# Sums by TensorE in five chunks only, a weight matrix stored by column group, and a new order, in a three-stage sequence kernel

## The chip, the cores and the metric

The kernel runs on one core of one Trainium2 chip. The metric is the device time of one execution in microseconds (us). The time of a version is the median of its runs.

## The reference, cut to what matters

The input has B = 4 sequences of S = 768 positions, H = 8 heads of D = 48 columns (8 * 48 = 384 = DM). Three stages follow one another.

```python
# 1: a recurrence with decay w and a bonus u, per head
cur   = outer(u * k[t], v[t])
y[t]  = r[t] @ (state + cur)
state = w[t][:, None] * state + outer(k[t], v[t])
# 2: four attention experts (64 columns each), two picked per position
a   = softmax(causal(scale * q_e @ k_e.T))
out += weight_e * (a @ v_e @ wo_e)
# 3: channel mix
xn  = (x - mu) / sqrt(var + 1e-6) * g_ln
out = x + relu(xn @ w_ch1) @ w_ch2        # 384 -> 1536 -> 384
```

Everything is float32; the kernel must stay near that precision, so most products are made from a high and a low float16 part of each operand, in three passes.

## The kernel before, in words

**Stage 1** (`rwkv_chunk`) works on chunks of 128 positions: 6 per sequence, 24 in all, numbered n = 6 b + c. Scans on VectorE make the running products of the decay (lines 801 and 816); TensorE then makes, per chunk, the matrix of products of r and k (`mm_a`, line 918, tile `pa`), the part of the output that comes from the state (`mm_inter`, line 954), the part within the chunk (`mm_intra`, lines 968 and 970) and the chunk's own addition to the state (`mm_d`, line 983, tile `pd`). A copy under a mask (`am_copy`, line 925) puts the products above the diagonal of the tile `am`, on whose diagonal GpSimd has written the bonus (`mk_bonus`, line 891).

The bonus of a position and head, sum over d of r k u, is made in one of two ways. For chunks n < NCB (8 before), GpSimd multiplies the transposed r and k of the chunk (`mk_rk`, line 847), TensorE sums over the partitions by 8 small matmuls against u (`mm_cb`, line 853, tile `pcb`) and ScalarE copies the 8 columns out (line 858). For the others, a transfer of 384 KB brings r and k by position (`load_q`, line 796, tile `tok`, of which there is one buffer), GpSimd multiplies them and then by u (lines 862 and 872), and VectorE sums (line 877). The u for this second way is loaded by `load_u` at chunk n = NCB.

The state goes from chunk to chunk in one of two ways as well. ScalarE multiplies the old state by the chunk's decay (`mk_dec`, line 910). Where `whole` is true (0 < c < 5 and n < NST, 10 before: chunks 1 to 4 and 7 to 9), TensorE adds that product to the chunk's own part in PSUM, by a matmul with the identity (line 979), and the next `mk_dec` reads the PSUM bank, which stays taken until then. In the other chunks two VectorE additions do it (line 998; copies at line 996 where c = 0), and the bank is free after them.

**Stage 2** (`project`, `attend`) makes q, k, v and the gates of a sequence (lines 1123 and 1188), the scores (line 1302), the softmax on ScalarE and VectorE, a transposing transfer, and the products with v and wo (lines 1387 and 1439).

**Stage 3** (`norm`, `mlp`) takes two blocks of 128 positions at a time: 18 matmuls per pair of column blocks with the first matrix (`mm_1`, line 1532, tile `pm`), 6 per step with the second (`mm_2`, line 1565, tile `pz`). There are 12 such pairs of blocks.

**The weights** w1 and w2 (each 384 x 1536 numbers) are read at the start as 64-bit words, because the matrices come as float64, in sets: w1 in 4 sets of 3 parts of 384 columns, w2 in 6 sets of 2 parts. VectorE unpacks a set in three passes over it (`decode`, lines 505, 506 and 507: `unpack` is a tensor_scalar, the other two are scalar_tensor_tensor). In the stored w1, part 4 kk + f holds row block kk and column group f, so that a set (one f, three kk) takes every fourth place. ScalarE takes the square sum of a set for its scale (line 575), and each part is then split in a high and a low half (lines 632 to 667; for w1 by a matmul with a diagonal, line 655).

**What sets the order.** All engines' instructions are written in one order worked out before compilation by `Plan.order`. It simulates the engines with the duration written beside each operation (`@op("PE", 0.85, ...)`). At each step it takes the operations that could start within LOOK of the earliest one of an engine, and among them the one with the smallest due time plus LATE times its delay; due times are sums of the entries of the table PLACE for the operation's group and name. Buffers come in rings (SIZES, for instance `tok=1`, PSUM ring `r=3`). Until the time UNTIL it may put in spare matmuls that only keep TensorE awake (`spin`, line 744), by the rule of SPAN, LEAST and GAP. So a change of PLACE or of a written duration changes the order of instructions on every engine and in SyncE's queue of transfers.

Of the kernel before, what the change touches and what calls it, by code (L numbers as in the profile page):

```python
# [20 lines left out]
P = 128  # L21
# [5 lines left out]
KK = DM // P  # L27
# [10 lines left out]
PRM = dict(LOOK=0.0, LATE=1773.6262, UNTIL=43.8356, SPAN=6.2999, LEAST=0.0732, GAP=2.1085, LAND=2.27, NPA=6, NQ=1, NCB=8, DIRECT=('w2',), NST=10)  # L38
PLACE = {
# [21 lines left out]
    ('o', 3, 5): -698477.53, ('proj', 0): -295018.27, ('proj', 0, 's'): -125022.81, ('proj', 0, 1): 80220.25,  # L61
    ('proj', 0, 2): -21343.01, ('proj', 1): -177643.56, ('proj', 1, 1): -107377.99, ('proj', 1, 2): -196040.46,
    ('proj', 2): -91098.53, ('proj', 2, 1): 13642.21, ('proj', 2, 2): -449346.82, ('proj', 3): 93391.83,
# [12 lines left out]
    ('vals', 0, 1): 35417.3, ('vals', 0, 2): -24875.8, ('vals', 1): -89872.89, ('vals', 2): 21146.28,  # L76
# [7 lines left out]
    ('w2', 8): 67189.64, 'a_den': -27933.93, 'a_hi': -151558.33, 'a_lo': 225945.59, 'a_of': -8012.47,  # L84
    'a_sum': 90213.0, 'a_tr': -81147.68, 'ae': 9532.96, 'am_copy': 126573.78, 'f_flag': -83856.37,
    'f_rows': 359040.86, 'f_turn': 39994.68, 'f_w': 28227.87, 'forth': 248281.69, 'g_exp': 19442.15,
    'g_norm': -38900.58, 'g_peak': -151938.75, 'g_rank': 230355.43, 'hi': 134007.83, 'less': -136319.44,
    'lo': -225283.24, 'load': -122866.37, 'load_g': -30043.72, 'load_k': -57046.71, 'load_q': -279458.56,
    'load_r': -217492.83, 'load_u': -13561.36, 'load_ut': 56724.36, 'load_v': 141804.62, 'm_hi': -262991.62,
    'm_lo': 122988.52, 'm_out': -32307.81, 'm_store': 132697.31, 'mk': 33523.95, 'mk_begin': 34263.89,  # L90
    'mk_bonus': -306653.38, 'mk_cb': -154529.96, 'mk_dec': -93213.35, 'mk_diag': -197725.73, 'mk_k2': 294244.16,
    'mk_k2t': 81775.2, 'mk_rk': -143861.49, 'mk_rp': -291319.24, 'mk_ruk': -96442.3, 'mk_sd': -340521.47,
    'mk_side': 120524.29, 'mk_tot': 228284.39, 'mm_1': 319489.06, 'mm_2': 191970.76, 'mm_a': -77276.6,
    'mm_av': -163565.22, 'mm_cb': 11831.02, 'mm_d': -269837.93, 'mm_inter': -24853.46, 'mm_intra': -48830.3,
    'mm_k': -8197.28, 'mm_o': 142200.91, 'mm_q': -177202.8, 'mm_s': -59954.25, 'mm_v': -130717.65, 'mt': -15383.65,
    'n_hi': -5943.82, 'n_lo': -146399.19, 'n_root': -31312.6, 'n_tr': 121898.14, 'n_var': -147654.16,
    'n_xn': -111826.26, 'o1': 140934.93, 'o2': -234884.57, 'o3': 6748.89, 'o4': -239856.13, 'o5': 93661.14,
    'o_mean': 273629.77, 'o_st': 120380.94, 'o_x1': -222100.87, 'q_hi': 140529.69, 'q_less': 98224.57,
    'q_lo': 97584.28, 's_bias': -108185.03, 's_exp': 5623.4, 's_hi': 119074.81, 's_lo': 11657.8, 's_max': 72228.32,
    's_tr': 53618.26, 'scan': 180273.48, 'se': -288101.94, 'stack_k': 117902.0, 'stack_q': 35533.64,  # L100
    'state': -226076.38, 'times': 63945.68, 'top': 19104.78, 'unpack': -157479.11, 'unpack2': 157371.31,
    'unpack3': 101864.41, 'v_hi': 188866.74, 'v_lg': -140728.23, 'v_lo': 25317.14, 'vc': -144449.83,
    'w_check': 22598.42, 'w_sane': 282903.73, 'ws_hi': 30208.09, 'ws_less': -128406.54, 'ws_lo': -66728.24,
# [200 lines left out]
NR = KK * DF // RW  # L304
# [1454 lines left out]
```

## Time and profile before

| | |
|---|---|
| median of 3 runs | 630.76 us (630.12 to 631.0) |
| the profiled execution's own time | 629.59 us |
| its span | 627.3 us |
| TensorE (PE) busy | 598.3 us, 95% of the span |
| VectorE (DVE) busy | 427.4 us, 68% |
| ScalarE (ACT) busy | 386.0 us, 62% |
| GpSimd (POOL) busy | 140.1 us, 22% |

The span is the time from the first to the last recorded instruction, and 2.3 us of the execution lie around it. PEld is TensorE's loading of weights, which overlaps its matmuls. A group of instructions is named by its line, engine and operation, with the tiles it writes and reads; L853 is line 853. PEclk is the clock that TensorE was granted, 1.00 being 2.4 GHz and 0.50 being 1.2 GHz.

### The profile page before, as it was taken

The numbers are of one execution on the slowest core, as the hardware profiler recorded it, in microseconds if no ns is written. First come the engines' busy times: TensorE is split into PE (matmuls) and PEld (weight loads), VectorE is DVE, ScalarE is ACT, GpSimd is POOL, SyncE is SP. The second block draws the span as 40 slices with busy tenths as digits, with TensorE's granted clock in tenths as the row PEclk, the third lists the DMA queues.
The fourth block names the chain that finished last, engine by engine and source line by source line (L and its number), as shares of the span: only waits on it lengthen the run. The fifth ranks groups of instructions, "written<-read, shape, count | busy, mean of one in ns | idle before, by whom it ended". The sixth has DMA issues, their size and how long they took to land.

```text
span 627.3 us, 16254 instructions
## 1 busy us (share of the span) xinstructions
PE 598.3 (95%) x6593; PEld 440.9 (70%) x6594; DVE 427.4 (68%) x808; ACT 386.0 (62%) x1062; POOL 140.1 (22%) x176
## 2 busy tenths in 40 slices
PE   6589899899999999999999999999999999999996
PEld 3357566677668866876877676776886768687783
DVE  5978788988978588888874898674464555542220
ACT  5367889876765586776656777573464756343120
POOL 4613043333644034325400232000000000000000
PEclk8659999899999999999999999999999999999999
DMA  8623764698996488739754767626228454522000
GB/s 279 228 101 124 191 168 128 130 226 212 193 215 123 93 217 162 186 81 248 168 84 103 194 128 162 112 56 121 48 43 152 93 102 85 100 62 60 14 14 31
DMA packets 150706, 82.15 MB, mean 131 GB/s; under 512 B 123616, under 2 KB 136672, under 8 KB 150624
## 3 DMA queue, kind: packets, MB, share of 16 engines
q1 hardware_dynamic: 150624, 81.03, 56.5%
q8 instruction: 54, 0.88, 0.6%
q14 instruction: 28, 0.23, 0.1%
HBM read 41.16 MB, written 4.72 MB: 73 GB/s over the span
## 4 chain that ended last, share of the span: by engine, by line
PE 72%; ACT 12%; DVE 10%; issue 3%; DMA 2%; SPq 0%; POOL 0%; ACTq 0%; DVEq 0%
PE pz L1565 21%; PE pm L1532 18%; PE pq L1123 7%; PE ps L1302 5%; PE po L1387 4%; PE px L1439 3%; ACT ps L1344 3%; PE pa L918 3%; PE py L968 2%; PE py L954 2%; PE pv L1188 1%; PE pk L936 1%; ACT hl L1360 1%; PE pd L983 1%; DMA xnT<-in_w_dram 1%
## 5 line engine op out<-in xcount | busy, mean ns | idle before, releaser
L1565 PE MATMUL pz<-w_w,hid 128*128 128x384 f16 x864 | 151.0, 326 | 0.2 <-DVE hid L1547 0.2
L1532 PE MATMUL pm<-xnT,w_w 128*128 128x256 f16 x1296 | 149.9, 273 | 0.2 <-DVE hid L1547 0.2
L1532 PEld LDWEIGHTS <-w_w 128*128 128x128 f16 x1296 | 124.8, 98 | 17.1 <-issue 1.7
L1565 PEld LDWEIGHTS <-hid 128*128 128x128 f16 x864 | 81.9, 98 | 50.7 <-issue 1.8
L1364 DVE SCALAR_TENSOR_TENSOR hl<-ps,hl 128x512 f16<-128x512 f32 (+2 forms) x68 | 54.7, 812 | 33.7 <-ACT hl L1360 33.0
L1547 DVE SCALAR_TENSOR_TENSOR hid<-pm,hid 128x512 f16<-128x512 f32 x72 | 49.3, 687 | 37.7 <-ACT hid L1543 37.6
L1543 ACT ACTIVATE hid<-pm 128x512 f16<-128x512 f32 x72 | 42.8, 594 | 50.8 <-PE pm L1532 50.7
L1481 POOL TENSOR_TENSOR rs_y<-rs_v,half 128x2 f32<-128x2 f32 x12 | 9.4, 780 | 229.6 <-ACT rs_v L1477 229.6
L1123 PE MATMUL pq<-xT,w_qk 128*128 128x256 f16 x432 | 51.8, 273 | 0.5 <-ACT qs L1148 0.5
L1360 ACT ACTIVATE hl<-ps 128x512 f16<-128x512 f32 (+2 forms) x68 | 46.7, 696 | 4.9 <-DMA pt<-hl 3.6
L1344 ACT ACTIVATE ps<-ps,bias 128x640 f32<-128x640 f32 (+1 forms) x32 | 26.2, 820 | 37.1 <-DVE ps L1315 34.1
L1123 PEld LDWEIGHTS <-w_qk 128*128 128x128 f16 x432 | 41.7, 98 | 6.9 <-issue 1.3
L891 POOL TENSOR_SCALAR_AFFINE_SELECT am<-cb 128x512 f32<-128x512 f32 x48 | 34.7, 745 | 40.2 <-DVE cb L877 26.2
L833 POOL TENSOR_TENSOR rp<-seq,fw 128x512 f32<-128x512 f32 x24 | 30.6, 1273 | 51.0 <-DVE fw L816 42.5
L1387 PEld LDWEIGHTS <-pt 128*128 128x128 f16 x1008 | 37.2, 99 | 5.6 <-DMA pt<-hl 1.0
L1387 PE MATMUL po<-vt,pt 128*128 128x64 f16 x1008 | 40.3, 194 | 0.6 <-DMA pt<-hl 0.5
L1572 DVE SCALAR_TENSOR_TENSOR x<-pz,ioutFalse,x 128x384 f32<-128x384 f32 x24 | 14.7, 614 | 36.7 <-PE pz L1565 36.7
L1315 DVE TENSOR_SCALAR_CACHE_REDUCE ps<-ps,scales 128x640 f32<-128x640 f32 (+1 forms) x32 | 30.6, 956 | 12.8 <-PE ps L1305 12.7
L1344 ACT ACTIVATE ps<-ps,bias,scales 128x128 f32<-128x128 f32 (+3 forms) x64 | 37.9, 591 | 1.8
L925 DVE COPY_PREDICATED am<-above,pa 128x512 f32<-128x512 int8 x48 | 33.0, 723 | 4.3 <-PE pa L918 4.2
L801 DVE TENSOR_TENSOR_SCAN bw<-seq,starts 128x516 f32<-128x516 f32 x24 | 30.9, 1288 | 1.5 <-DMA seq<-in_seq_dram 1.5
L918 PE MATMUL pa<-rp,k 48*128 48x128 f32 x384 | 29.6, 290 | 1.7 <-DVE dec L996 1.6
(225 smaller groups left out, 1060.0 us busy)
## 6 DMA issues: line engine op xcount, KB each, us to landing
seq<-in_seq_dram SPq DMA_DIRECT2D x48, 256.0 KB, 4.0
seq<-in_seq_dram SPq DMA_DIRECT2D x24, 258.5 KB, 3.3
tok<-in_tok_dram SPq DMA_DIRECT2D x16, 384.0 KB, 4.0
seq<-in_seq_dram SPq DMA_DIRECT2D x24, 192.0 KB, 4.0
xnT<-in_w_dram SPq DMA_DIRECT2D x6, 768.0 KB, 4.4
x<-in_w_dram SPq DMA_DIRECT2D x4, 1152.0 KB, 7.2
out_dram<-x SPq DMA_DIRECT2D x24, 192.0 KB, 2.6
xk<-kd SPq DMA_DIRECT2D x16, 192.0 KB, 4.2
```

The costliest lines, as they stand in the source:

```text
L891: G.affine_select(out=t["am"][:, j], in_=t["cb"].rearrange("p (h j) -> p h j", j=2)[:, :, j, None].to_broadcast([P, NP, P]), compare_op=OP ...
L918: T.matmul(t["pa"][j][:, hp * P : (hp + 1) * P], t["k2"][o : o + D, hp, :], t["rp"][o : o + D, hp, :], start=True, stop=True)
L925: V.copy_predicated(t["am"][:, j], above[:, None, :].to_broadcast([P, NP, P]), t["pa"][j].rearrange("p (h t) -> p h t", t=P))
L1123: T.matmul(h["pq"][:, :n].rearrange("p (c t) -> p c t", t=P), wt["qk"][:, lw, kk, mt * P : (mt + 1) * P], t["xT", c0 // 2][:, :, lx * KK + ...
L1344: A.activation(ps, ps, AF.Exp, bias=h["bias"][:, e : e + 1], scale=-1.0 if alone else t["x"]["esc"], accum_out=r["sums"][:, e : e + 1])
L1360: A.activation(part(u, heads, 0, W), view(heads, h, W, spot), AF.Copy, scale=2.0 ** 14)
L1364: V.scalar_tensor_tensor(out=part(u, heads, half_at, W), in0=view(heads, h, W, spot), scalar=2.0 ** 14, in1=part(u, heads, 0, W), op0=OP.m ...
L1387: T.matmul(r["po"][:, e * HD : (e + 1) * HD], u["pt"][:, (lp * len(heads) + k) * (i + 1) + kb, :], t["vt"][:, kb, lv, e * HD : (e + 1) * H ...
L1532: T.matmul(h["pm"][:, j * 256 : (j + 1) * 256].rearrange("p (c t) -> p c t", t=P), wt["w1"][:, 4 * kk + f // 3, lw, f % 3 * P : (f % 3 + 1 ...
L1543: A.activation(hid[fp][:, 0], h["pm"], AF.Relu)
L1547: V.scalar_tensor_tensor(out=hid[fp][:, 1], in0=h["pm"], scalar=0.0, in1=hid[fp][:, 0], op0=OP.max, op1=OP.subtract)
L1565: T.matmul(h["po"][:, :DM], hid[fp][:, lh, c0 : c0 + P], wt["w2"][:, 2 * fp + j, lw, :], start=(fp + j + i == 0), stop=(fp == NF // 2 - 1 ...
```

## The change

NCB goes from 8 to 5 and NST from 10 to 5. So chunks 5, 6 and 7 make their bonuses from `tok`, and chunks 7, 8 and 9 add their state on VectorE; chunks 0 to 4 (bonuses) and 1 to 4 (states) stay on TensorE. In the stored w1, part 3 f + kk now holds column group f and row block kk: a set is three neighbouring parts, and the destination of its unpacking is contiguous, while the same data are read from memory into the same buffer. The written duration of `unpack` changes with it. The settings of the planner and the whole of PLACE are new. The matmuls that read w1 have the same shapes as before.

```diff
-PRM = dict(LOOK=0.0, LATE=1773.6262, UNTIL=43.8356, SPAN=6.2999, LEAST=0.0732, GAP=2.1085, LAND=2.27, NPA=6, NQ=1, NCB=8, DIRECT=('w2',), NST=10)
+PRM = dict(LOOK=0.0326, LATE=14146.9836, UNTIL=35.809, SPAN=5.4007, LEAST=0.144, GAP=2.97, LAND=2.3828, NPA=6, NQ=1, NCB=5, DIRECT=('w2',), NST=5)
 PLACE = {
-    ('av', 0, 0): 47055.04, ('av', 0, 1): -203728.69, ('av', 0, 2): -46772.52, ('av', 0, 3): -134002.41,
...
+    ('av', 0, 0): -158057.83, ('av', 0, 1): -232158.2, ('av', 0, 2): -102859.22, ('av', 0, 3): -263757.53,
...
-    SETS = dict(w1=[[4 * kk + f for kk in range(KK)] for f in range(4)], w2=[[2 * j, 2 * j + 1] for j in range(NR // 2)])
+    SETS = dict(w1=[[KK * f + kk for kk in range(KK)] for f in range(4)], w2=[[2 * j, 2 * j + 1] for j in range(NR // 2)])
...
-                pick = slice(some[0], some[-1] + 1, some[1] - some[0])
+                pick = slice(some[0], some[-1] + 1)
+                src = slice(k, None, 4) if which == "w1" else pick
...
-                def load(pick=pick, flat=flat, ring=ring, hold=hold, n=n, direct=direct):
+                def load(pick=src, flat=flat, ring=ring, hold=hold, n=n, direct=direct):
...
-                @op("V", n * 0.4 + 0.06, after=[load], follow=[dec])
+                @op("V", n * 0.21 + 0.14, after=[load], follow=[dec])
                 def unpack(hold=hold):
...
-                    kk = part * KK // NR
+                    kk = part % KK
...
-                @op("PE", 0.98, after=[q["ready"]] + [big_done["w1"][4 * kk + (2 * fp + j) // 3] for kk in range(KK)], follow=[mms[-1] if mms else pe],
+                @op("PE", 0.98, after=[q["ready"]] + [big_done["w1"][KK * ((2 * fp + j) // 3) + kk] for kk in range(KK)], follow=[mms[-1] if mms else pe],
...
-                                     wt["w1"][:, 4 * kk + f // 3, lw, f % 3 * P : (f % 3 + 1) * P], q["xnT"][:, :, lx * KK + kk, :],
+                                     wt["w1"][:, KK * (f // 3) + kk, lw, f % 3 * P : (f % 3 + 1) * P], q["xnT"][:, :, lx * KK + kk, :],
```

## Rows read from the trace of the kernel before

**Rows 1.** The page, part 1: busy time, share, instructions of each engine.

```profile
PE 598.3 (95%) x6593; PEld 440.9 (70%) x6594; DVE 427.4 (68%) x808; ACT 386.0 (62%) x1062; POOL 140.1 (22%) x176
```

**Rows 2.** Busy time by stage: us, then PE, PEld, DVE, ACT, POOL, PEclk, DMA share, GB/s.

```profile
0.00:48.00 48.00, 33.16 (x235) 20.16 (x236) 35.91 (x80) 25.61 (x86) 20.70 (x32) 0.68 0.62 205
48.00:80.00 32.00, 29.25 (x323) 19.73 (x323) 26.99 (x46) 26.77 (x81) 5.45 (x6) 1.00 0.52 153
80.00:128.00 48.00, 44.23 (x506) 31.72 (x504) 43.07 (x88) 43.40 (x132) 19.80 (x22) 0.96 0.60 143
128.00:160.00 32.00, 30.97 (x473) 23.54 (x472) 28.13 (x45) 21.88 (x60) 10.89 (x14) 1.00 1.01 224
160.00:300.00 140.00, 139.48 (x1778) 104.43 (x1776) 114.52 (x206) 97.19 (x272) 55.31 (x64) 1.00 0.77 170
300.00:620.00 320.00, 319.13 (x3281) 240.19 (x3279) 178.18 (x344) 171.11 (x436) 27.92 (x41) 1.00 0.45 92
620.00:627.30 7.30, 2.11 (x13) 1.08 (x11) 0.62 (x1) 0.00 (x0) 0.00 (x0) 0.79 0.11 36
```

**Rows 3.** Waits of PE from 48 to 160 us, the longest: total, times, longest.

```profile
PE pa L918 <- DVE dec L996: 1.6, 1, 1.6
```

**Rows 4.** The chain of waits in the first 62 us: start, us, what.

```profile
23.28 1.26 DVE w_w L506
...
35.51 1.26 DVE w_w L505
```

**Rows 5.** Timeline of PE, 80 to 130 us: start, us, what.

```profile
99.85 0.95 PE L853 MATMUL pcb<-ut,rk 128*128 128x2 f32 x8
100.66 0.89 PE L655 MATMUL w_ps_False<-w_w,diag_w_False 128*128 128x384 f32 x2
...
128.10 2.13 PE L1532 MATMUL pm<-xnT,w_w 128*128 128x256 f16 x18
```

**Rows 6.** Timeline of PE, 130 to 165 us.

```profile
136.59 0.89 PE L979 MATMUL pd<-dec,ident 128*128 128x384 f32 x2
137.40 0.56 PE L983 MATMUL pd<-seq,k2t 128*48 128x48 f32 x16
```

**Rows 7.** Instructions of line 505: count, ns min/median/max, first and last start, form.

```profile
L505 DVE TENSOR_SCALAR w_w<-xnT x6: 551/627/984, 15.1 to 111.1; 128x768 int32<-128x768 int32 x6
L505 DVE TENSOR_SCALAR w_w<-x x4: 1340/1344/1348, 21.2 to 74.3; 128x1152 int32<-128x1152 int32 x4
```

**Rows 8.** Groups on DVE, shapes apart: busy us, mean ns, idle before.

```profile
L877 DVE TENSOR_REDUCE cb<-tok 128x8 f32<-128x384 f32 x16 | 8.7, 544 | 0.0
...
L998 DVE TENSOR_TENSOR dec<-dec,pd 48x192 f32<-48x192 f32 x18 | 6.3, 349 | 2.0 <-PE pd L983 1.7
```

**Rows 9.** Groups on PE and POOL: busy us, mean ns, idle before.

```profile
L862 POOL TENSOR_TENSOR tok<-tok 128x384 f32<-128x384 f32 x16 | 17.2, 1076 | 52.7 <-DMA tok<-in_tok_dram 52.7
L872 POOL TENSOR_TENSOR tok<-tok,u_sb 128x384 f32<-128x384 f32 x16 | 17.1, 1068 | 0.9
...
L847 POOL TENSOR_TENSOR rk<-seq 128x512 f32<-128x512 f32 x8 | 13.2, 1654 | 44.9 <-DMA seq<-in_seq_dram 44.9
...
L744 PE MATMUL spin<-starts,ident 128*128 128x512 bf16 x13 | 6.7, 609 | 2.9 <-POOL ident masks.py:199 2.1 <-PE pcb L853 0.5
```

**Rows 10.** The page, part 6: DMA issues, KB each, us to landing.

```profile
tok<-in_tok_dram SPq DMA_DIRECT2D x16, 384.0 KB, 4.0
```

**Rows 11.** Waits of the whole span, one of POOL: total, times, longest.

```profile
POOL tok L862 <- DMA tok<-in_tok_dram: 52.7, 13, 13.0
```

**Rows 12.** Busy time by microsecond around 113 us, columns as in group 2.

```profile
113.00:114.00 1.00, 0.00 (x0) 0.00 (x0) 1.00 (x2) 0.98 (x2) 0.00 (x0) 1.00 1.12 207
114.00:115.00 1.00, 0.43 (x7) 0.46 (x9) 0.95 (x4) 1.00 (x3) 0.00 (x0) 1.00 0.94 197
...
116.00:117.00 1.00, 1.00 (x7) 0.69 (x5) 1.00 (x2) 1.00 (x3) 0.00 (x0) 0.50 0.91 286
...
119.00:120.00 1.00, 0.94 (x8) 0.68 (x7) 1.00 (x3) 0.97 (x6) 1.00 (x1) 0.96 0.00 0
```

More of the change, by code (lines that the diff above doesn't have):

```diff
@@ L36 @@
 PACK = OFF_TV + DM
-PRM = dict(LOOK=0.0, LATE=1773.6262, UNTIL=43.8356, SPAN=6.2999, LEAST=0.0732, GAP=2.1085, LAND=2.27, NPA=6, NQ=1, NCB=8, DIRECT=('w2',), NST=10)
+PRM = dict(LOOK=0.0326, LATE=14146.9836, UNTIL=35.809, SPAN=5.4007, LEAST=0.144, GAP=2.97, LAND=2.3828, NPA=6, NQ=1, NCB=5, DIRECT=('w2',), NST=5)
 PLACE = {
[21 rows of a table removed]
-    ('o', 3, 5): -698477.53, ('proj', 0): -295018.27, ('proj', 0, 's'): -125022.81, ('proj', 0, 1): 80220.25,
-    ('proj', 0, 2): -21343.01, ('proj', 1): -177643.56, ('proj', 1, 1): -107377.99, ('proj', 1, 2): -196040.46,
-    ('proj', 2): -91098.53, ('proj', 2, 1): 13642.21, ('proj', 2, 2): -449346.82, ('proj', 3): 93391.83,
[12 rows of a table removed]
-    ('vals', 0, 1): 35417.3, ('vals', 0, 2): -24875.8, ('vals', 1): -89872.89, ('vals', 2): 21146.28,
[7 rows of a table removed]
[L84 to L103, printed above, removed]
-    'ws_load': 66852.66, 'ws_times': -17374.3, 'ws_top': -348457.17, 'x_hi': -14285.97, 'x_lo': 26889.45,
-    'x_rest': -61247.9, 'xabs': -182346.53,
[21 rows of a table added]
+    ('o', 3, 5): -887226.63, ('proj', 0): -273674.18, ('proj', 0, 's'): -122947.25, ('proj', 0, 1): 33967.49,
+    ('proj', 0, 2): -22865.81, ('proj', 1): -161669.97, ('proj', 1, 1): -124244.76, ('proj', 1, 2): -170937.04,
+    ('proj', 2): -240584.25, ('proj', 2, 1): -133453.44, ('proj', 2, 2): -618311.36, ('proj', 3): -265444.39,
[12 rows of a table added]
+    ('vals', 0, 1): 167679.1, ('vals', 0, 2): 134570.26, ('vals', 1): 116604.02, ('vals', 2): 138180.09,
[7 rows of a table added]
+    ('w2', 6): 52773.5, ('w2', 8): 31100.68, 'a_den': 14387.47, 'a_hi': -226014.08, 'a_lo': 119853.05,
+    'a_of': 14990.11, 'a_sum': -23005.87, 'a_tr': -86486.52, 'ae': 13364.87, 'am_copy': 101284.17, 'f_flag': 6249.28,
+    'f_rows': 336025.77, 'f_turn': 211916.52, 'f_w': 27592.3, 'forth': 238007.75, 'g_exp': 96727.16,
+    'g_norm': -74813.54, 'g_peak': -284005.22, 'g_rank': 163327.52, 'hi': 155788.23, 'less': -154816.0,
+    'lo': -285324.76, 'load': -135288.75, 'load_g': -64407.03, 'load_k': -1204.15, 'load_q': -138492.93,
+    'load_r': -202067.16, 'load_u': -35451.52, 'load_ut': 199504.57, 'load_v': 163165.8, 'm_hi': -259670.45,
+    'm_lo': 156385.77, 'm_out': -793.17, 'm_store': -2232.31, 'mk': -26467.94, 'mk_begin': -20494.19,
+    'mk_bonus': -285109.93, 'mk_cb': -168933.44, 'mk_dec': 24474.69, 'mk_diag': -156582.35, 'mk_k2': 311735.47,
+    'mk_k2t': 69840.01, 'mk_rk': -56760.49, 'mk_rp': -171197.22, 'mk_ruk': -121790.73, 'mk_sd': -273117.05,
+    'mk_side': 62504.08, 'mk_tot': 255960.68, 'mm_1': 209632.69, 'mm_2': 154285.28, 'mm_a': -132133.18,
+    'mm_av': -230430.05, 'mm_cb': -11847.17, 'mm_d': -201747.42, 'mm_inter': -12283.48, 'mm_intra': -105157.35,
+    'mm_k': 38115.05, 'mm_o': 182366.02, 'mm_q': -84489.5, 'mm_s': -121907.74, 'mm_v': -277668.69, 'mt': -54669.57,
+    'n_hi': 249586.43, 'n_lo': -196801.04, 'n_root': -88352.01, 'n_tr': 90347.4, 'n_var': -209277.23,
+    'n_xn': -38449.7, 'o1': 105423.18, 'o2': -302686.95, 'o3': 119306.42, 'o4': -275877.1, 'o5': 60929.99,
+    'o_mean': 275559.74, 'o_st': 151884.12, 'o_x1': -232643.29, 'q_hi': -58960.13, 'q_less': 121980.76,
+    'q_lo': 83580.24, 's_bias': -95372.35, 's_exp': 63370.7, 's_hi': 225991.02, 's_lo': 102552.12, 's_max': 127395.92,
+    's_tr': 238166.37, 'scan': 199743.38, 'se': -233207.23, 'stack_k': 26188.59, 'stack_q': 41739.5,
+    'state': -377626.84, 'times': 39319.26, 'top': 41000.02, 'unpack': -188646.78, 'unpack2': 189437.25,
+    'unpack3': 121387.77, 'v_hi': 114737.05, 'v_lg': -164014.86, 'v_lo': -31620.69, 'vc': -264859.07,
+    'w_check': 38915.34, 'w_sane': 322124.85, 'ws_hi': 112064.32, 'ws_less': -21291.52, 'ws_lo': -110984.31,
+    'ws_load': 4387.61, 'ws_times': -92221.94, 'ws_top': -461471.1, 'x_hi': -29107.52, 'x_lo': 33016.11,
+    'x_rest': -231804.15, 'xabs': -247472.5,
@@ L654, in times @@
                     hold["ps"] = bank("m", f"{which}_ps{part}_{safe}")[:, :RW]
-                    T.matmul(hold["ps"], diags[which][:, part * KK // NR if which == "w1" else 0], full[:, part], start=True, stop=True)
+                    T.matmul(hold["ps"], diags[which][:, part % KK if which == "w1" else 0], full[:, part], start=True, stop=True)
                 @op("A", 0.49, after=[times, tops[which][part]])
```

78 rows, old and new, of the table PLACE are left out of this document.

## The prediction

> **What bounds the kernel now.** The page's first part comes first: TensorE is busy in 598.3 of 627.3 us [rows 1]. So the time is TensorE's work plus 29.0 us in which it stands, and an edit pays if it takes work from TensorE without making it stand longer. The second view, busy time by stage, says where it stands [rows 2]: 14.8 us in the first 48, 2.8 us from 48 to 80, 3.8 us from 80 to 128, 1.0 us from 128 to 160, 1.4 us in the 460 us after that, and 5.2 us at the very end, behind the last matmul. From 160 us on there is always a matmul ready; work taken away before that time lets all the rest come earlier, if the gap is filled. The same rows show a second loss: in the first 48 us the granted clock is 0.68 on the mean. The third view, TensorE's waits between 48 and 160 us, lists eleven kinds; the longest is 1.6 us [rows 3], and none of the eleven is for a bonus or for a state that TensorE did not sum. Last, the chain of the first 62 us runs mostly over VectorE's unpacking of the weights, for instance an unpack at 35.51 us [rows 4].
>
> **The change part by part.** *Bonuses of chunks 5, 6 and 7.* A group of 8 small matmuls leaves TensorE. Its row says 0.95 us, but the next matmul starts 0.81 us after it [rows 5], and that is the place it takes in the queue. The three groups begin at 99.85, 108.15 and 122.92 us, of nearly equal length: 3 * 0.81 = 2.4 us less work.
>
> *States of chunks 7, 8 and 9.* Two matmuls with the identity leave TensorE in each; from their start to the next instruction's it is 137.40 - 136.59 = 0.81 us [rows 6]; the other two are alike. Again 2.4 us less. The 16 matmuls behind them stay. Together TensorE loses 4.8 us of work.
>
> *Unpacking of w1.* Four instructions over three strided parts take 1.344 us each; the same operation over two neighbouring parts of w2 takes 0.551 to 0.984, median 0.627 us [rows 7]. For three neighbouring parts no row exists. The bounds are 1.5 times the quickest, 0.83 us, and no change, 1.34 us; I take 1.5 times the median, 0.94 us, since that row is the nearest in operation and form. That is 0.4 us less, four times. The unpacking at 35.51 us is on the chain [rows 4] and counts 0.4 us. The first, at 21.2 us, is not: the chain enters at the step behind it, at 23.28 us. The other two start after 48 us, where VectorE is busy in 27.0 of 32 us [rows 2], and count nothing. The two other passes over each set, and the split of the parts, keep their shapes.
>
> *What VectorE gets.* Three sums of 0.544 us and, for three states, two additions of 0.349 us each [rows 8]: 1.6 + 2.1 = 3.7 us. It stands 4.9 us between 80 and 128 and 3.9 us between 128 and 160 us [rows 2]. From 160 to 300 us it does the same operations, is busy in 114.5 of 140 us, and TensorE stands only 0.5 us. So the states, which fall behind 128 us, cost nothing. The bonuses fall before, where no channel-mix matmul is there to fill a gap (the first starts at 128.10 us [rows 5]) and VectorE, at 90%, would be at 93%. Bounds: nothing, and all 1.6 us; I take half, 0.8 us, because ScalarE, at 43.4 of 48 us, is no less full and gets nothing from this.
>
> *What GpSimd gets.* Two multiplications by position (1.076 and 1.068 us) for one transposed (1.654 us) [rows 9]: 0.5 us more per chunk, 1.5 in all. It is busy in 19.8 of the 48 us, so this costs nothing while the tokens arrive in time. But its queue is in order: behind a multiplication that waits for tokens stand the chunk's product for `pa`, the side copy and the bonuses, and behind these the masked copy and TensorE's products within the chunk.
>
> *Transfers.* SyncE's queue issues three more loads of 384 KB, each 4.0 us to landing [rows 10], and the load of u (192 KB) moves from chunk 8 to chunk 5: 1.34 MB more in a stage that moves 143 GB/s and uses 60% of the DMA engines. All must pass the one queue that also issues the chunks' loads and the transposes. I count nothing in the sum and keep the price for a rival.
>
> *PSUM banks.* In chunks 7 to 9 the bank of the state is free after the additions and not only after the next chunk's scaling. TensorE has no wait of note for a bank there [rows 3], so nothing. The next scaling reads SBUF in place of PSUM, also nothing.
>
> *The order.* PLACE, the planner's settings and its spare matmuls are all new, and no row shows the new order. Bounds: TensorE is busy 33.2 us in the first 48 [rows 2], of which 6.7 are spare matmuls [rows 9]; the other 26.5 us at a clock of 0.68 hold 18.0 us of work at full clock. A start that kept the clock up would win at most 8.5 us; one that is as much worse loses about that. For the sum I take zero, as the start's instructions, all in chunks 0 to 3 and the weights, are almost the same ones.
>
> The sum: -4.8 (TensorE) - 0.4 (unpack) + 0.8 (sums on VectorE) = -4.4 us. The profiled execution took 629.6 us, so 625.2 us. The median of the runs shown is 1.2 us above that execution; I put the forecast a little up for it, at **625.5 us**, which is 0.8% under that median.
>
> **The rivals.** *Late tokens, slower.* Over the span GpSimd waited 52.7 us in 13 places for tokens, 4.05 us each [rows 11]. Those places lie where channel-mix matmuls fill TensorE. Moved to chunks 5 to 7, before 128 us, such a wait holds up what I listed behind it, and TensorE has little else. With all three uncovered: 629.6 - 4.8 - 0.4 + 12.2 = 636.6 us. It turns the sign once more than (4.8 + 0.4) / 3 = 1.7 us per chunk reach TensorE. For it speaks the single token buffer: a load can't be issued before the last sum is made. Against it, GpSimd is idle in most of this stage, and no wait for a bonus is seen on TensorE after 48 us [rows 3]. Chance 0.20.
>
> *The clock falls once more, no change.* At 113 us TensorE stood for 1.57 us; two microseconds later its clock went to 0.50 and came back at 119 us [rows 12]. Between 115 and 119 us that cost about 0.2 + 3 * 0.5 = 1.7 us. The same stage now loses 2.4 us of TensorE's work, without channel-mix matmuls to put in. If the gaps stay empty and bring one more such fall, only the states pay: 629.6 - 2.4 - 0.4 + 0.8 + 1.7 = 629.3 us, no change. The Trainium skill says on its page "TensorE: Matmul & The Clock Gate", section "HAM oscillation — how this bites in real kernels", that gaps between bursts of matmuls put the clock back and that the loss is paid again at each; the trace agrees with that around 113 us (0.50), and by it alone taking small matmuls out of a thin stage would bring this rival's 629.3 us and not my 625.5. Chance 0.14, because the stage's clock was full in all but those four microseconds, and matmuls of projections, weights and scores stand directly behind the bonuses [rows 5] and can move up.
>
> *A better start.* If the new order gets about half of the 8.5 us of the slow clock back, 625.5 - 4.2 = 621.3 us. For it: there is much to win. Against: the chain there is VectorE's and ScalarE's, not TensorE's. Chance 0.16.
>
> **How the numbers follow.** The forecast has 0.50, and its own range is 622 to 629 us: the two halves of the VectorE bound, the unpack's bounds and some microseconds of the order. The better start (0.16) is faster, the fallen clock (0.14) is mostly no change, 0.10, and else slower, late tokens (0.20) are slower. A measurement of this kernel tells about 0.2%, 1.3 us, from no change. So faster 0.66, same 0.10, slower 0.24. The range reaches from 618 us, where all but 1 us of the slow clock's 8.5 us is won on top, to 634 us, where two thirds of the late tokens are uncovered (629.6 - 5.2 + 8.1 + 1.2 for the median); I leave out about 0.05 below and 0.13 above.
>
> **What would show it.** In the changed profile line 853 has 40 matmuls (64 before) and line 979 has 8 (14 before); lines 862 and 877 count 19, line 998 counts 24. Right: TensorE busy about 5 us less, its idle time near 29 us, unpacks of w1 under 1 us, TensorE full from 160 us or earlier. Wrong: waits of GpSimd for tokens between 80 and 128 us with TensorE idle above 5 us there (late tokens); a second stretch at 0.50 after 48 us (the clock); TensorE's loss in the first 48 us changed by more than 3 us either way, which would mean that the order decides and not the sums.

## The result, and the profile after

The changed kernel takes **625.17 us** (median of 4 runs, 624.58 to 626.55) where the kernel before, run beside it, takes 630.88 us: the ratio is 0.9916 [0.9896, 0.9936] (the quotient of the two medians is 0.9909). The profile is of a run of 624.58 us with a span of 622.9 us, 4.4 us less than before. In the changed file the lines behind about line 549 have a number higher by one.

First part of the page of the changed kernel, busy time by engine:

```profile
PE 591.2 (95%) x6560; PEld 438.1 (70%) x6560; DVE 431.1 (69%) x817; ACT 386.8 (62%) x1059; POOL 153.9 (25%) x179
```

Against [rows 1] TensorE has lost 7.1 us of work, but it stands 622.9 - 591.2 = 31.7 us in place of 29.0: 2.7 us of the work taken away have become idle time, and 7.1 - 2.7 is the 4.4 us of the span. Not all of the 7.1 us are sums: the spare matmuls are 10 where they were 13, 5.2 us in place of the 6.7 of [rows 9]. Where it stands is read from the changed kernel's busy time by stage, with the columns of [rows 2]:

```profile
0.00:48.00 48.00, 35.91 (x287) 25.05 (x288) 38.65 (x87) 28.93 (x96) 22.03 (x32) 1.00 0.69 234
48.00:80.00 32.00, 28.03 (x324) 19.57 (x323) 28.61 (x58) 26.68 (x86) 11.28 (x13) 1.00 0.51 160
80.00:128.00 48.00, 40.13 (x438) 26.25 (x441) 42.74 (x78) 40.63 (x119) 17.36 (x17) 0.96 0.65 161
128.00:160.00 32.00, 31.99 (x457) 24.47 (x449) 26.64 (x45) 22.35 (x60) 12.27 (x13) 1.00 0.80 191
160.00:300.00 140.00, 139.10 (x1817) 106.29 (x1816) 116.50 (x210) 98.18 (x267) 55.46 (x63) 1.00 0.75 167
300.00:620.00 320.00, 316.03 (x3257) 236.43 (x3253) 177.93 (x344) 170.01 (x435) 35.56 (x43) 1.00 0.47 93
```

The first 48 us lose 2.7 us of idle time (12.1 for 14.8), but the stretch from 80 to 128 us gains 4.1 (7.9 for 3.8), and that is where the bonuses left TensorE. From 128 us on it is full. (The clock of 1.00 in the first row has no record behind it before 35 us: see the last section.)

Groups of instructions of the changed kernel, busy time and mean, and under them the unpacking by its line (minimum, median and maximum in ns, first and last start):

```profile
L854 PE MATMUL pcb<-ut,rk 128*128 128x2 f32 x40 | 7.4, 308 | 0.0
L980 PE MATMUL pd<-dec,ident 128*128 128x384 f32 x8 | 3.4, 503 | 0.0
```

```profile
L505 DVE TENSOR_SCALAR w_w<-x x4: 736/749/928, 20.9 to 68.7; 128x1152 int32<-128x1152 int32 x4
```

The counts are those foretold (40 and 8). The two groups had 9.5 us in 64 and 6.9 us in 14 instructions, so 2.1 and 3.5 us of matmul time have gone. The four unpacks of w1 take 0.749 us in the median, where [rows 7] has 1.344 in the kernel before.

Waits between 48 and 160 us in the changed kernel, total, times and longest, of TensorE:

```profile
PE ps L1303 <- DVE hl L1365: 2.9, 3, 1.2
PE pq L1145 <- ACT kd L1138: 2.2, 2, 2.0
PE pv L1189 <- DVE sane L679: 1.6, 1, 1.6
...
PE py L955 <- DVE am L926: 0.2, 1, 0.2
```

and of GpSimd:

```profile
POOL tok L863 <- DMA tok<-in_tok_dram: 23.6, 3, 13.3
```

GpSimd waits 23.6 us for tokens here, in three places, but of all that is queued behind it TensorE feels one wait of 0.2 us for a masked matrix. TensorE's longest waits are others: VectorE's high and low parts of the scores' softmax (`ps`, whose single buffer in PSUM they free) and ScalarE's queries and keys.

At last the timeline of TensorE, the products `pa` of the chunks. Before:

```profile
46.94 1.16 PE L918 MATMUL pa<-rp,k 48*128 48x128 f32 x16
67.22 1.60 PE L918 MATMUL pa<-rp,k 48*128 48x128 f32 x16
```

After, with the first channel-mix matmul:

```profile
44.73 1.27 PE L919 MATMUL pa<-rp,k 48*128 48x128 f32 x16
62.44 1.73 PE L919 MATMUL pa<-rp,k 48*128 48x128 f32 x16 [0.21 <-DVE vt L1204]
...
122.75 3.06 PE L1533 MATMUL pm<-xnT,w_w 128*128 128x256 f16 x18
```

Chunk 2 is ahead by 2.2 us, chunk 3 by 67.22 - 62.44 = 4.8 us, and the first channel-mix matmul by 128.10 - 122.75 = 5.4 us [rows 5]. **In these two profiles the whole gain stands at 62 us**, some 35 us ahead of the first place where a sum left TensorE. Behind chunk 3 the two orders differ too much to compare chunk by chunk, but the rest can be compared as a whole. From the start of chunk 3 to the end the kernel before takes 560.1 us and the changed one 560.5:

```profile
67.22:627.30 560.08, 547.25 (x6185) 407.89 (x6184) 376.10 (x709) 345.19 (x934) 114.40 (x140) 0.99 0.58 125
62.44:622.90 560.46, 542.23 (x6136) 403.54 (x6136) 378.76 (x715) 346.20 (x928) 124.72 (x142) 1.00 0.57 125
```

TensorE has 547.25 - 542.23 = 5.0 us less work in this rest, about what the sums were to bring, and stands 18.2 us in it instead of 12.8. So behind 62 us the work taken off went into idle time.

### The profile page after: what moved, and what is told of

Read it like the earlier page. It is cut to its first block, busy times and chain, and to the rows that moved or that the text cites. A ratio compares the mean times of both kernels' runs of the same rounds, so it can differ in the third digit from the quotient of the medians.

```text
span 622.9 us, 16217 instructions
## 1 busy us (share of the span) xinstructions
PE 591.2 (95%) x6560; PEld 438.1 (70%) x6560; DVE 431.1 (69%) x817; ACT 386.8 (62%) x1059; POOL 153.9 (25%) x179
## 4 chain that ended last, share of the span: by engine, by line
PE 72%; DVE 11%; ACT 9%; DMA 4%; issue 2%; SPq 1%; POOL 0%; ACTq 0%; DVEq 0%
PE pz L1566 21%; PE pm L1533 21%; PE pq L1124 6%; PE ps L1303 5%; PE po L1388 4%; PE pa L919 3%; PE px L1440 3%; PE py L969 2%; PE pv L1189 2%; DMA xnT<-in_w_dram 2%; PE py L955 2%; ACT ps L1345 2%; DMA seq<-in_seq_dram 1%; DVE hl L1365 1%; PE pd L984 1%
## 5 line engine op out<-in xcount | busy, mean ns | idle before, releaser
L892 POOL TENSOR_SCALAR_AFFINE_SELECT am<-cb 128x512 f32<-128x512 f32 x48 | 44.7, 954 | 60.8 <-DVE cb L878 37.7
L863 POOL TENSOR_TENSOR tok<-tok 128x384 f32<-128x384 f32 x19 | 22.5, 1182 | 84.9 <-DMA tok<-in_tok_dram 84.9
L802 DVE TENSOR_TENSOR_SCAN bw<-seq,starts 128x516 f32<-128x516 f32 x24 | 35.4, 1476 | 0.8 <-DMA seq<-in_seq_dram 0.6
```

The lines of the kernel that those rows point to most:

```text
L802: V.tensor_tensor_scan(t["bw"][:, NP * CW : 0 : -1], t["wT"][:, NP * CW : 0 : -1], starts[:, NP * CW : 0 : -1], 0.0, op0=OP.mult, op1=OP.max)
L892: G.affine_select(out=t["am"][:, j], in_=t["cb"].rearrange("p (h j) -> p h j", j=2)[:, :, j, None].to_broadcast([P, NP, P]), compare_op=OP ...
```

## The experiments

All were timed in five rounds against runs of the kernel before on the same chip. A difference to the changed kernel is the difference of two ratios times 630.5 us; the changed kernel's ratio is the mean of its two measurements, (0.9916 + 0.9926) / 2 = 0.9921. Such a difference is uncertain by 1.3 to 1.7 us, as each ratio is by about 0.002.

**The changed kernel again.** No edit.

> The changed kernel once more, as the measure for the runs beside it and to see how far its start repeats. All theories: 625 us, 5 to 6 us under the kernel before. What is open is the clock at the start: in the profiles on hand TensorE's matmuls come to full length at 35 us in the changed kernel and at 44 us in the one before. If that belongs to the program, it shows at 35 us again, within one or two us; if it is chance of an execution, it moves by several us.

Measured: 626.17 us, 0.9926 [0.9906, 0.9945]. So the change is worth (1 - 0.9921) * 630.5 = 5.0 us. The start repeats: the first clock record of this profile is at 36.0 us, that of the changed kernel's first profile at 35.0 us.

**The new order's table with the old sums and the old layout**, planned anew from that table.

```diff
-PRM = dict(LOOK=0.0326, LATE=14146.9836, UNTIL=35.809, SPAN=5.4007, LEAST=0.144, GAP=2.97, LAND=2.3828, NPA=6, NQ=1, NCB=5, DIRECT=('w2',), NST=5)
+PRM = dict(LOOK=0.0326, LATE=14146.9836, UNTIL=35.809, SPAN=5.4007, LEAST=0.144, GAP=2.97, LAND=2.3828, NPA=6, NQ=1, NCB=8, DIRECT=('w2',), NST=10)
...
-    SETS = dict(w1=[[KK * f + kk for kk in range(KK)] for f in range(4)], w2=[[2 * j, 2 * j + 1] for j in range(NR // 2)])
+    SETS = dict(w1=[[4 * kk + f for kk in range(KK)] for f in range(4)], w2=[[2 * j, 2 * j + 1] for j in range(NR // 2)])
...
```

> The changed kernel with bonuses on TensorE for eight chunks and states for chunks up to nine again: what stays of the change is the new table, the planner's settings and the stored w1. Theory of work (TensorE has 4.8 us less to do and the order is worth nothing): the gain goes but for 0.4 us, 629 to 630 us. Rival of order (the gain comes from the new start): 625 to 626 us. A planner that was led off its course by the eight and ten chunks would give more than 631 us.

**Ten states on TensorE again, planned anew** (`NST=5` to `NST=10`).

> The changed kernel with the states of chunks 7 to 9 summed by TensorE again (bonuses stay at five chunks). Theory of work: 3 * 0.81 = 2.4 us more, 627.5 us. Rival of order: 625 us. If the PSUM bank that then stays taken matters, more than 628 us.

**Eight bonuses on TensorE again, planned anew** (`NCB=5` to `NCB=8`).

> The changed kernel with the bonuses of chunks 5 to 7 summed by TensorE again (states stay at five chunks). Theory of work: 2.4 us more on TensorE and 0.8 us back from VectorE, 626.8 us. Rival of order: 625 us. If the late tokens that GpSimd is seen to wait for cost anything (23.6 us of its waiting before 160 us), this is faster than the changed kernel, 621 to 624 us.

Measured: 671.36 us, 1.064 [1.0618, 1.0662]; 633.04 us, 1.0047 [1.003, 1.0064]; 646.07 us, 1.0256 [1.0231, 1.028]. No theory of mine had such sizes: 8 to 45 us above the changed kernel, for 2.4 us of matmuls or twice that. The stages of the first of the three show where:

```profile
128.00:160.00 32.00, 20.36 (x258) 13.81 (x257) 21.45 (x33) 21.19 (x58) 10.70 (x10) 0.84 0.82 192
160.00:300.00 140.00, 135.59 (x1694) 103.25 (x1693) 107.26 (x194) 93.25 (x252) 40.55 (x46) 0.99 0.70 145
300.00:620.00 320.00, 308.93 (x3310) 230.61 (x3306) 188.93 (x355) 171.41 (x446) 48.07 (x60) 0.98 0.48 103
```

TensorE stands 11.6 us between 128 and 160 us, where before it stands one, and every other engine is less busy there too: they wait for one another. It stands another 4.4 and 11.1 us in the two stages behind. The planner, given other operations and the same table, had written out another order. These three runs tell what an order is worth and nothing about a sum. All runs behind them but one keep the order of the kernel that they start from, instruction by instruction.

**The state's sums put back as extra work, order kept.**

```diff
+                if 7 <= n <= 9:
+                    T.matmul(t["pd"][:, :DM], ident, u_sb, start=True, stop=True, skip_group_check=True)
```

> The changed kernel in its own order, instruction for instruction, with one more matmul with the identity (two records, 0.81 us) in front of the state's part in chunks 7, 8 and 9, whose result is overwritten. It measures what TensorE's work costs at that place, without a new order. Theory of work: 3 * 0.81 = 2.4 us more, 627.6 us. Rival (the gaps there take it up): 625.2 us.

Measured: 628.11 us, 0.9964 [0.9949, 0.998], so (0.9964 - 0.9921) * 630.5 = 2.7 us for work forecast at 2.4.

**The bonuses' matmuls put back as extra work, order kept.**

```diff
+            if 5 <= n <= 7:
+                for hp in range(NP):
+                    T.matmul(t["pa"][0][:, 2 * hp : 2 * hp + 2], t["rp"][:, hp, :], ut[:, hp, :], start=True, stop=True)
```

> The changed kernel in its own order, with four more two-column float32 matmuls (8 records, 0.81 us) in front of the products of r and k in chunks 5, 6 and 7, whose result is overwritten. Theory of work: 2.4 us more, 627.6 us. My sum took 0.8 us off for a stage that is not TensorE's alone, so 1.6 to 2.4. Rival (TensorE stands 7.9 us in that stage and takes it up): 0 to 0.8 us.

Measured: 627.89 us, 0.9967 [0.995, 0.9984], so 2.9 us for work forecast at 2.4. In the new order, then, work added to TensorE before 160 us costs its full length, as far as an uncertainty of some 1.4 us tells.

**The old layout of w1 in the changed kernel, order kept.**

```diff
-    SETS = dict(w1=[[KK * f + kk for kk in range(KK)] for f in range(4)], w2=[[2 * j, 2 * j + 1] for j in range(NR // 2)])
+    SETS = dict(w1=[[4 * kk + f for kk in range(KK)] for f in range(4)], w2=[[2 * j, 2 * j + 1] for j in range(NR // 2)])
...
-                pick = slice(some[0], some[-1] + 1)
+                pick = slice(some[0], some[-1] + 1, some[1] - some[0])
...
```

> The changed kernel in its own order, with w1 stored as before (a set takes every fourth place), so that only the four unpackings of w1 are longer: 1.344 in place of 0.749 us. If only the one on the chain counts, 0.6 us more, 625.8 us. If all four do, 2.4 us, 627.6 us. If none, 625.2 us.

Measured: 626.8 us, 0.9948 [0.9928, 0.9969], so 1.7 us, uncertain by 1.5. Its unpacks, by their line, are those of before again, 2.2 us longer in all than in the changed kernel. And a wait stands in its profile that no profile of the changed kernel has, that of TensorE's split of a part of w1 for VectorE's unpacking:

```profile
L505 DVE TENSOR_SCALAR w_w<-x x4: 1335/1339/1345, 21.1 to 69.0; 128x1152 int32<-128x1152 int32 x4
PE w_ps_False L664 <- DVE w_w L506: 0.9, 1, 0.9
```

**The new layout in the kernel before, its own order** (the same edit the other way).

> The kernel before in its own order, with w1 stored by column group: only the four unpackings are shorter, by 0.6 us each. If only the one on its chain at 35.5 us counts, 630.2 us; if all four, 628.4 us; if the time so won is lost again at the next wait, 630.8 us.

Measured: 627.16 us, 0.9961 [0.9941, 0.9981]: the layout alone is worth (1 - 0.9961) * 630.5 = 2.5 us, half of the whole gain. Its timeline of TensorE has chunk 3 at

```profile
65.36 1.60 PE L919 MATMUL pa<-rp,k 48*128 48x128 f32 x16
```

which is 1.9 us ahead of the 67.22 us of before. The time is not explained by shorter unpacks alone. In this profile the four take 0.842, 1.179, 1.743 and 0.748 us, 0.9 us less in all than before and not 2.4:

```profile
L505 DVE TENSOR_SCALAR w_w<-x x4: 748/1010/1743, 21.4 to 72.4; 128x1152 int32<-128x1152 int32 x4
```

And the lead is there at chunk 2 already (45.09 us for 46.94), when two of them have saved 0.7 us. What else went is a set of waits. In the kernel before, the chain of [rows 4] runs on behind the unpack at 35.51 us as

```profile
37.53 1.28 DVE w_w L506
...
38.89 0.50 ACT w_w L659
39.42 1.37 DVE w_w L507
40.83 0.48 PE w_ps_False L663
```

Lines 506 and 507 unpack the second set there, lines 659 and 663 split a part of the first. By the program a split needs its own set alone, but here the split and the unpacking wait for one another, TensorE at last 1.68 us. With the new layout the same matmul waits for nothing:

```profile
40.83 0.48 PE L663 MATMUL w_ps_False<-w_w,minus 128*128 128x384 f16 x1 [1.68 <-DVE w_w L507]
39.19 0.32 PE L664 MATMUL w_ps_False<-w_w,minus 128*128 128x384 f16 x1
```

All four profiled kernels with strided sets have waits of a split for the unpacking, and none of the ten with neighbouring parts has one. In a strided layout the parts of one set lie between those of another in the tile `w_w`; that this is why they are made to wait is argued from the edit, not shown. How the 2.5 us divide between the shorter pass and the waits is open. This profile is also of one of the longer runs (629.49 us, 2.3 above the median), and its lead has shrunk to 0.2 us by the end; the 2.5 us rest on the medians.

**VectorE's and GpSimd's new work made small in the changed kernel, order kept.** For chunks 5 to 7 the tokens' transfer, products and sum, and for chunks 7 to 9 the additions of the state, cover a quarter of their columns.

```diff
-                V.tensor_reduce(out=t["cb"], in_=t["q"][:, 0].rearrange("p (h d) -> p h d", d=D), axis=AX.X, op=OP.add)
+                V.tensor_reduce(out=t["cb"], in_=t["q"][:, 0, : t["qw"]].rearrange("p (h d) -> p h d", h=H), axis=AX.X, op=OP.add)
...
-                        V.tensor_tensor(out=dst, in0=dst, in1=pdv[rows], op=OP.add)
+                        V.tensor_tensor(out=dst[:, :, :e], in0=dst[:, :, :e], in1=pdv[rows][:, :, :e], op=OP.add)
```

> The changed kernel in its own order, with what VectorE, GpSimd and the transfers got made light: in chunks 5 to 7 the tokens, their two products and their sums cover a quarter of the columns, and in chunks 7 to 9 the additions to the state a quarter of theirs; the rest of the bonuses and states is left out. About 2.3 us less on VectorE, 4.8 us on GpSimd, 0.9 MB less to load. TensorE's work and all waits are as before. If VectorE's new sums cost what my sum says (0.8 us) or all of their 3.7 us, this is 0.8 to 2.3 us faster than the changed kernel, 0.988 to 0.991 of the kernel before. If late tokens cost, more than that. If the new work is hidden, as the additions were forecast to be, 0.992.

The rest of those bonuses and states is left out. Measured: 624.43 us, 0.9911 [0.9888, 0.9934]: 0.6 us under the changed kernel, uncertain by 1.7. So the new work costs 2.3 us at most, and the 12.2 us of late tokens are excluded; nothing and the 0.8 us of the forecast are not told apart. The run bears on another question as well, since its start has a slow clock until 40 us:

```profile
36.00:40.00 4.00, 3.64 (x10) 2.02 (x9) 3.96 (x6) 3.31 (x11) 0.00 (x0) 0.50 0.00 0
40.00:44.00 4.00, 4.00 (x40) 3.00 (x40) 2.83 (x5) 3.00 (x9) 1.54 (x1) 0.94 0.95 309
```

The clock of the changed kernel's own profile came up by 35.0 us, of the kernel before at 44.0 us. Here it came 5 us later than in the first, and the execution took 624.79 us, 0.4 more than the median. Over all 50 runs in the changed kernel's order (its own and those of the four other experiments that keep it) the 17 with a mean clock under 0.99, to which this execution belongs, took 0.7 us more than the other runs of the same kernels, uncertain by 0.7. (In the profiles of this order a clock up at 40 or 41 us goes with a mean of 0.985 or 0.987, one up by 35 or 36 us with 0.996 to 0.999.) So a clock that comes up 5 us later costs about that much.

**TensorE's sums made short in the kernel before, its own order.** This takes off in place, and without new work elsewhere, most of what the change takes off: the identity matmuls of chunks 7 to 9 in one pass over constants, and one matmul over eight columns (two records for eight) in the bonuses of chunks 5 to 7. The state of the chunk before and three quarters of the bonus are left out there.

```diff
+                if n >= 5:
+                    T.matmul(t["pcb"][:, :H], t["rk"][:, 0, :], ut.rearrange("p h j -> p (h j)"), start=True, stop=True)
-                for hp in range(NP):
+                for hp in range(NP if n < 5 else 0):
...
+                    if n >= 7:
+                        T.matmul(t["pd"][:, : NP * wide], ident16, starts[:, : NP * wide], start=True, stop=False, skip_group_check=True)
```

> The kernel before in its own order, with TensorE's sums made light: in chunks 7 to 9 the identity matmul in float32 gives way to one in bfloat16 over constants (0.16 in place of 0.81 us), in chunks 5 to 7 the four float32 matmuls of the bonus to one over eight columns (0.2 in place of 0.81 us). The state of the chunk before and three quarters of the bonus are left out there. About 3 * 0.65 + 3 * 0.6 = 3.8 us less on TensorE, nothing else moves. Theory of work: 626.3 us, 0.994 of the kernel before. If the gaps between 80 and 128 us belong to other engines, the bonuses give nothing and 2 us remain, 0.997.

Measured: 629.75 us, 0.9991 [0.9976, 1.0007]: **0.6 us**, uncertain by 1.0 and so not told from nothing. Its stages from 80 to 160 us:

```profile
80.00:128.00 48.00, 41.22 (x465) 28.84 (x461) 44.15 (x86) 41.57 (x125) 18.02 (x21) 0.96 0.56 138
128.00:160.00 32.00, 30.87 (x501) 24.37 (x494) 28.66 (x48) 23.67 (x67) 11.25 (x14) 1.00 1.02 227
```

Against [rows 2] TensorE loses 44.23 - 41.22 = 3.0 us of work from 80 to 128 us and stands 6.8 us instead of 3.8. The bonuses are 2.0 of the 3.0 us, and the rest is matmuls that start only behind 128 us here; nothing moved up to fill the gap. VectorE is now busy in 44.15 of those 48 us. Two of TensorE's waits from 48 to 160 us say what is late next,

```profile
PE ps L1307 <- DVE hl L1369: 2.7, 3, 1.1
PE pa L920 <- DVE dec L1001: 1.6, 1, 1.6
```

both on VectorE: that for the buffer of the scores has grown, the other is as long as in [rows 3]. In the kernel before the first of them was

```profile
PE ps L1302 <- DVE hl L1364: 0.9, 2, 0.5
```

And the timeline has the first channel-mix matmul not earlier but 1.9 us later than the 128.10 us of [rows 5]:

```profile
130.01 2.24 PE L1537 MATMUL pm<-xnT,w_w 128*128 128x256 f16 x19
```

**The due times nudged.** The changed kernel's operations, none added or removed; each entry of the table from which the due times are summed is moved by up to 1000 either way (the entries lie between about -1,400,000 and 550,000), and the order planned anew.

```diff
+PLACE = {k: v + 1000.0 * (zlib.crc32(repr(k).encode()) % 2001 / 1000.0 - 1.0) for k, v in PLACE.items()}
```

> The changed kernel with every entry of its table moved by up to 1000 either way, about half a per cent of a common entry: the same operations in another order. If any order by nearly this table does (my sum set the order at zero), 0.990 to 0.996 of the kernel before. If the table is fitted to one order, so that the re-planned kernels with eight or ten chunks lost 8, 21 and 46 us by the order alone, it is slower than the changed kernel by several us, 1.00 or more.

Measured: 657.57 us, 1.0435 [1.0412, 1.0457]: (1.0435 - 0.9921) * 630.5 = 32 us for the same work in another order. Between 128 and 160 us TensorE stands again, 7.1 us, and the clock is 0.73:

```profile
128.00:160.00 32.00, 24.90 (x340) 18.36 (x330) 24.44 (x41) 21.83 (x59) 14.26 (x13) 0.73 0.81 179
```

**Layout and short sums together in the kernel before, its own order.**

> The kernel before in its own order with both: w1 stored by column group as in the run of the layout alone, which gave 0.9961, and TensorE's sums light as in the run of the light sums alone, which gave 0.9991 (the state of the chunk before in chunks 7 to 9 and three quarters of the bonus in chunks 5 to 7 are left out). If VectorE's unpacking was what kept TensorE's saved work from counting, the sums now pay: 3 us and more on top of the layout, 0.989 to 0.992. If other waits of the old order hold it, nothing is added to the layout, 0.995 to 0.996, and the rest of the change's gain, to 0.992, came with the new order and not with the work taken off.

Measured: 627.12 us, 0.9933 [0.9907, 0.9959]. With the layout alone at 0.9961, the short sums add (0.9961 - 0.9933) * 630.5 = 1.8 us here, uncertain by about 2. It lies between the two expectations and tells them not apart. Against the kernel before, the two together are worth (1 - 0.9933) * 630.5 = 4.2 us in the old order, uncertain by 1.6: most of the change's 5.0.

No run was quicker than the changed kernel by more than is uncertain. The new order with the old sums, instruction by instruction as the changed kernel has it, wasn't tried otherwise than by extra work.

## Why the prediction was right, and where its steps were not

The number (625.5 for 625.17) and the sign were right, and the sum of -4.4 us stands beside 5.0 measured. That they agree so closely is in part luck: one term was far too small and another, in the order that the prediction looked at, too large, and the two errors nearly cancel.

**The unpacking was mis-sized.** The step "0.4 us less, four times", of which one counts, gave -0.4 us; measured are 1.7 us (taken from the changed kernel) and 2.5 us (given to the one before). The price of one was 0.749 us and not 0.94: the time does not go with the size from the strided or the median row, and the lower bound of 0.83 was not low enough either. But the price is not the whole error. The step took the layout for a matter of the length of one instruction, and left out that the split of one set and the unpacking of the next waited for one another, although the chain of [rows 4] ran through those waits behind the very unpack that it counted. They are gone in every profile with the new layout.

**The sums were rightly priced and doubtfully counted.** "Work taken away before that time lets all the rest come earlier, if the gap is filled" rests on TensorE's 95%. In the order of before the gap was not filled: sums shortened in place gave 0.6 us, with VectorE's release of the buffer of the scores as the next wait, and beside the new layout 1.8 us, uncertain by 2. In the new order the same work, put back, costs its full price, 2.7 and 2.9 us for 2.4 forecast each, but in the two profiles the work that left behind 62 us became idle time. So 0.81 us per group was right as a price; whether it is paid depends on the order around it.

One reading was wrong on the way: of TensorE's waits, "none of the eleven is for a bonus or for a state that TensorE did not sum". The longest of them, 1.6 us [rows 3], is put down to line 996, by which VectorE copies just such a state out of PSUM where c = 0.

**"Order: 0" was wrong as a statement.** An order planned anew from the same numbers moves the time by 8 to 45 us, and one from a nudged table by 32 us. A zero with bounds of 8.5 us from the slow clock alone looked at the wrong place: the price of an order is in the waits of the engines for one another, from 128 us on as well (and, in the nudged one, in a granted clock of 0.73 there). The term may have come out small because this order was written for this set of operations; no run shows the reason. Counted from the kernel before, the parts give 2.5 + 0.6 = 3.1 us one by one and 4.2 us together; counted from the changed one 1.7 + 2.7 + 2.9 = 7.3 us (uncertain by some 3); the change itself gave 5.0. It is not shown to be additive, and **how the 2.5 us beyond the layout divide** between the sums and the order is left open.

**VectorE's +0.8 us** is neither confirmed nor refuted: with the new sums and additions cut to a quarter of their columns the time fell by 0.6 us, uncertain by 1.7. **GpSimd, transfers and banks at nothing** held within the same uncertainty: the waits for tokens are there and TensorE feels 0.2 us of what is queued behind them, although GpSimd's busy time grew by 13.8 us against [rows 1] where I had counted 3 * 0.5 = 1.5. The rest is mostly longer instructions, for instance its masks, 954 ns each in place of 745; it had the room.

**The rivals.** *Late tokens*: the sign that the prediction set for them was met as written, since GpSimd waits for tokens between 80 and 128 us (4.0 us at one place) while TensorE stands 7.9 us there, above the 5. The sign was a poor one. TensorE's waits behind the masks are 0.2 us, and with the tokens cut to a quarter the time fell by 0.6 us and not by 12. *The clock falls once more* did not come: one fall, as before, now at 124 us,

```profile
123.00:124.00 1.00, 1.00 (x11) 0.85 (x9) 0.59 (x1) 1.00 (x3) 0.00 (x0) 0.88 0.29 68
124.00:125.00 1.00, 1.00 (x7) 0.67 (x6) 1.00 (x4) 0.35 (x2) 0.00 (x0) 0.50 0.84 183
```

but its premise, gaps that stay empty when small matmuls leave a thin stage, was true: 4.1 us more idle time there. *A better start* comes nearest to what happened, as the lead is there by 62 us, but hardly by way of the clock: where it rose at about 40 us and not at 35, the runs took 0.7 us longer, not 4.2. TensorE's idle time in the first 48 us fell by 2.7 us, just short of the 3 at which the prediction would have said that the order decides. Of its signs of being right, the unpacks under 1 us and TensorE full from 160 us held; TensorE lost 7.1 us of work and not 5, and stands 31.7 us, not 29.

## What to carry to other kernels

An engine at 95% need not pace the stage in which it is relieved: shorten the work in place, in the same order, and see whether the time or the idle time takes it up, before counting it. A written-out order belongs to its set of operations; hold it fixed while a part is tested, since planning anew can cost ten times the part. And when the parts of a tile are laid out anew, look for waits between engines that come or go with it, and not only at the length of the instruction that writes them.

## What the runs showed that was not expected

**A strided destination nearly doubles a pass of VectorE over one source.** 1152 words per partition take 0.749 us into a contiguous destination and 1.344 us into three parts, with nothing else changed. The Trainium skill, page "VectorE: DVE Perf Modes", section "What auto-detection actually checks", gives twice the rate to an instruction with one source if source and destination lie in SBUF and their outermost dimensions are both even or equal. A destination of three parts beside a source in one row of 1152 is neither, and the trace's ratio of 1344 / 749 = 1.8 agrees with it.

**The quick form is the one that GpSimd can stretch.** In the kernel before with the new layout, one of the four unpacks took 1.74 us. The timeline of VectorE,

```profile
51.71 1.74 DVE L505 TENSOR_SCALAR w_w<-x 128x1152 int32<-128x1152 int32 x1
```

and of GpSimd at that time:

```profile
51.29 1.55 POOL L834 TENSOR_TENSOR rp<-seq,fw 128x512 f32<-128x512 f32 x1 [4.88 <-PE ws_ps L734]
52.95 2.70 POOL L892 TENSOR_SCALAR_AFFINE_SELECT am<-cb 128x512 f32<-128x512 f32 x2
```

The two run side by side, and the unpack takes longer than the strided form (1.340 to 1.348 us in [rows 7]) ever did. In the kernel before, the strided unpack at 53.55 us ran beside the same multiplication (53.13 us, 1.55 us long) and took 1.348 us. That the overlap is the cause is argued from these rows, not tried.

**A clock of 1.00 can mean that none was recorded yet.** The first stage of the changed kernel shows 1.00, but its records of the clock begin at 35.0 us; ahead of that the same 16 matmuls take 2.08 us that take 1.27 and 1.16 later:

```profile
21.52 2.08 PE L919 MATMUL pa<-rp,k 48*128 48x128 f32 x16
44.73 1.27 PE L919 MATMUL pa<-rp,k 48*128 48x128 f32 x16
```

So durations of one kind of matmul tell the clock where the column doesn't.
